# A memory-attention and sticky-routing expert kernel: values of batch 1 loaded ahead of the choice, their products split around the first w1 products

## The chip, the cores and the metric

The kernel runs on one core of a Trainium2 chip. The time is the device time of one execution in microseconds (us); lower is better. The core has five engines that run side by side, each in its own program order: TensorE (PE, with its weight loads shown as PEld), VectorE (DVE), ScalarE (ACT), GpSimd (POOL) and SyncE (SP), which here only issues transfers. An engine waits at an instruction until the semaphores that the instruction names have come, and everything behind it on that engine waits with it. Transfers between HBM and the on-chip memory go through DMA queues that SP fills; nearly all go through one.

## What is computed

The reference is a linear-attention step whose output goes through a sparse expert layer, for 8 batches of 8 heads, 576 tokens, head size 64, 32 memories, 8 experts with a hidden size of 1024. Cut to what matters:

```python
a = exp(phi - max(phi, axis=2)); a = a / (sum(a, axis=2) + 1e-9)
k_m = einsum('bhsm,bhsd->bhmd', a, k)
v_m = einsum('bhsm,bhsd->bhmd', a, v)
scores = q @ k_m.T / sqrt(64)
attn = softmax(scores)                     # over the 32 memories
x = (attn @ v_m), heads side by side       # (B, 576, 512)
logits = x @ w_gate
# token s keeps the expert of token s-1 when its local gate is 0.5 or more, token 0 takes the best
out[b, s] = softmax(logits[b, s])[e] * (relu(x[b, s] @ w1[e]) @ w2[e])
```

Because of the rule on the previous token, the tokens of one batch mostly share the expert that token 0 chose. The kernel therefore runs each batch once through that one expert; pairs of a batch and a further expert are listed at the end and done in a loop, which is passed over with these inputs.

## The kernel before

The work of a batch has two halves. The attention half turns `phi` into weights (column maximum `cm`, turned and reduced to `mc`, spread back as `cx`, subtracted, exponential, column sums `asum`), multiplies them with keys and values (`pkv`, line 396, 72 small products in 64x32 tiles of PE, keys and values side by side), adds the column sums (`f_sums`, line 407, into the same PSUM tiles), scales and turns the result (`kvn`, `pT`, `kvT`), and then treats the queries in two parts of 9 blocks of 32 tokens, called a and z: turn the queries (`qT`), scores (`psc`), softmax on DVE and ACT (`sc`), turn the weights back (`at`), and split them into a coarse and a fine part (`ah` on ACT, `al` on POOL). The choice of the expert (`c_pl`, `c_choice`) needs only token 0; `expert` reads the number into SP, and only then can w1 and w2 of that expert be asked for.

The expert half folds the values' means into w1 (`pg`, line 787, then `Gh` on ACT and `Gl` on DVE), multiplies (`hidden`: `ph`, line 819, 6 products for each 128 hidden units, relu'd by ACT and DVE into `h`) and multiplies with w2 (`second` and `second_turned`: `po`). The `ph` tiles and the `pg` tiles share three PSUM buffers, so a tile waits until DVE has read the one three before it. `hidden` runs four tiles of 256 tokens for two chunks each, then eight tiles of 320 tokens.

While the expert half of batch b runs on PE, the attention half of batches b+1 and b+2 is strewn between its products. Where, is written in the table `PLACES`: for each step and batch a place on a time axis of the products alone (37.8 units for each batch); a step is issued on all its engines, SP included, when the loop has passed that place. I call the expert half of batch b stage b: stage 0 runs from about 28 us, stage 2 from about 138 us.

The first attention half has nothing to hide behind. `start` writes its order out by hand: all of batch 0's attention, the load of batch 1's `phi` and keys and values, part of batch 1's attention, and `warm(n)`, n dummy products on PE, where PE would stand idle. The first `pg` runs in two halves (`lo` and `hi`), for whose input w1's first half is loaded in two pieces.

Two more rules set waits. `at` has one buffer, so DVE can write the next batch's `at` only after the store `att_d` of the last one has read it. And the loads of keys and values, of `phi`, and of the queries have one buffer each.

## Time and profile before

| what | value |
|---|---|
| three runs | 414.85, 415.64, 418.31 us; median 415.64 us |
| the profiled execution | 416.56 us, span from first to last instruction 414.8 us |
| granted clock of TensorE, mean | 0.999 of full speed |
| PE busy | 95% of the span |
| DVE, ACT, POOL busy | 69%, 43%, 36% of the span |
| moved by DMA | 82.58 MB, 199 GB/s over the span |

The profile is one execution. "Busy" is the time in which an engine worked on an instruction; matmuls overlap, so a busy PE need not be at its peak. A wait is put down to what came last. Since PE is the fullest engine, idle time of the others costs nothing as long as PE does not wait for them.

### The profile page before, as it was taken

Reading aid. Unit: us, or ns where it says so; the run is one execution under the profiler, and the core shown is the slowest. Engines: PE = TensorE matmul, PEld = TensorE weight load, DVE = VectorE, ACT = ScalarE, POOL = GpSimd, SP = SyncE. Lnnn points to the kernel's source line nnn. Section 1 sums busy time; section 2 is a strip of 40 time slices with the busy share of each in tenths; the row PEclk is TensorE's granted clock in tenths of the full one; section 3 lists DMA queues with packets and bytes.
Section 4 is the critical chain, followed back from the end, with each engine's and each line's share of the span. In section 5 each row is a group of like instructions: output and inputs, shape, how many; then the busy total and the mean of one; then the engine's idle time right before and its main releaser. Section 6 shows DMA issues by size and latency. Waiting matters only on the chain.

```text
span 414.8 us, 10606 instructions
## 1 busy us (share of the span) xinstructions
PE 395.0 (95%) x4195; PEld 326.7 (79%) x4195; DVE 284.4 (69%) x714; ACT 177.8 (43%) x427; POOL 150.9 (36%) x162
## 2 busy tenths in 40 slices
PE   8778898999999989999999999999999999999994
PEld 2546866798777977699778997789878996899884
DVE  4487788878976797886759767777757676625300
ACT  2154652436442744435541564336541564146010
POOL 3024541536241744038510681029410660156000
PEclk9999999999999999999999999999999999999999
DMA  8969793999197939798789198965974087202011
GB/s 238 286 224 291 167 372 122 199 283 378 31 351 127 371 131 246 174 379 299 228 162 399 37 300 152 297 244 164 241 134 170 2 246 253 82 0 65 25 40 55
DMA packets 115445, 82.58 MB, mean 199 GB/s; under 512 B 69616, under 2 KB 89088, under 8 KB 115392
## 3 DMA queue, kind: packets, MB, share of 16 engines
q1 hardware_dynamic: 115328, 81.84, 66.4%
q8 instruction: 35, 0.57, 0.6%
q14 instruction: 18, 0.15, 0.1%
q0 software_dynamic: 64, 0.02, 0.1%
HBM read 66.60 MB, written 15.24 MB: 197 GB/s over the span
## 4 chain that ended last, share of the span: by engine, by line
PE 79%; DMA 11%; DVE 5%; issue 1%; SPq 1%; ACT 1%; DVEq 0%
PE ph L819 22%; PE po L907 8%; PE po L857 8%; PE po L908 7%; PE po L909 7%; PE po L859 7%; PE po L858 7%; DMA att_d<-at 6%; DMA kv_t<-in_v_dram 5%; PE pkv L396 4%; PE pg L787 3%; PE psc L507 2%; PE pl L604 1%; DVE h L829 1%; PE po L881 1%
## 5 line engine op out<-in xcount | busy, mean ns | idle before, releaser
L777 POOL TENSOR_TENSOR w2l<-raw,w2h 128x512 fp32r<-128x512 f32 x64 | 82.0, 1303 | 31.2 <-ACT w2h L776 23.5
L819 PE MATMUL ph<-ah,Gh 128*128 128x256 f32 (+1 forms) x256 | 74.5, 306 | 1.4 <-DVE h L829 1.3
L829 DVE SCALAR_TENSOR_TENSOR h<-ph,h 128x320 fp32r<-128x320 f32 (+2 forms) x104 | 52.7, 519 | 31.9 <-ACT h L827 31.5
L819 PE MATMUL ph<-ah,Gl 128*128 128x256 f32 (+1 forms) x256 | 71.6, 295 | 0.0
L907 PE MATMUL po<-h,w2l 128*128 128x320 f32 x224 | 71.5, 319 | 0.0
L909 PE MATMUL po<-h,w2h 128*128 128x320 f32 x224 | 69.2, 309 | 0.0
L908 PE MATMUL po<-h,w2h 128*128 128x320 f32 x224 | 69.2, 309 | 0.0
L827 ACT ACTIVATE h<-ph 128x320 fp32r<-128x320 f32 (+1 forms) x96 | 46.4, 489 | 44.7 <-PE ph L819 44.4
L857 PE MATMUL po<-w2h,h 128*128 128x512 f32 (+1 forms) x152 | 60.7, 399 | 0.0
L914 POOL TENSOR_TENSOR oT<-oT,gT 128x320 f32<-128x320 f32 x28 | 20.7, 741 | 104.3 <-DVE oT L913 97.4
L859 PE MATMUL po<-w2h,h 128*128 128x512 f32 (+1 forms) x152 | 57.8, 380 | 0.0
L858 PE MATMUL po<-w2l,h 128*128 128x512 f32 (+1 forms) x152 | 57.7, 379 | 0.0
L819 PE MATMUL ph<-al,Gh 128*128 128x256 f32 (+1 forms) x256 | 54.8, 295 | 0.0
L819 PEld LDWEIGHTS ph<-ah,Gh 128*128 128x128 f32 x256 | 48.1, 188 | 7.6 <-issue 3.6
L819 PEld LDWEIGHTS ph<-ah,Gl 128*128 128x128 f32 x256 | 48.2, 188 | 0.0
L563 POOL TENSOR_TENSOR al<-at,ah 128x576 fp32r<-128x576 f32 (+1 forms) x18 | 23.1, 1289 | 64.7 <-ACT ah L559 42.8
L907 PEld LDWEIGHTS po<-h,w2l 128*128 128x128 f32 x224 | 42.0, 188 | 5.6 <-issue 5.2
L776 ACT ACTIVATE w2h<-raw 128x512 fp32r<-128x512 f32 x64 | 38.4, 625 | 11.9 <-PE po L909 10.1
L908 PEld LDWEIGHTS po<-h,w2h 128*128 128x128 f32 x224 | 42.1, 188 | 0.2
L909 PEld LDWEIGHTS po<-h,w2h 128*128 128x128 f32 x224 | 42.1, 188 | 0.0
L819 PEld LDWEIGHTS ph<-al,Gh 128*128 128x128 f32 x256 | 41.1, 188 | 0.1
L857 PEld LDWEIGHTS po<-w2h,h 128*128 128x128 f32 x152 | 28.6, 188 | 14.3 <-issue 9.4
(153 smaller groups left out, 578.6 us busy)
## 6 DMA issues: line engine op xcount, KB each, us to landing
raw<-in_moe_w_dram SPq DMA_DIRECT2D x34, 512.0 KB, 6.2
raw<-in_moe_w_dram SPq DMA_DIRECT2D x15, 1024.0 KB, 6.9
kv_t<-in_k_dram SPq DMA_DIRECT2D x7, 1152.0 KB, 8.7
kv_t<-in_v_dram SPq DMA_DIRECT2D x7, 1152.0 KB, 11.2
q_t<-in_q_dram SPq DMA_DIRECT2D x112, 72.0 KB, 3.3
att_d<-at SPq DMA_DIRECT2D x8, 576.0 KB, 9.8
out_dram<-oT SPq DMA_DIRECT2D x28, 160.0 KB, 5.6
out_dram<-ot SPq DMA_DIRECT2D x17, 256.0 KB, 6.0
```

The lines of the kernel that those rows point to most:

```text
L563: (eng or nc.gpsimd).tensor_tensor(out=st.al[:, gs, ss], in0=st.at[:, gs, ss], in1=st.ah[:, gs, ss], op=ALU.subtract)
L776: nc.scalar.activation(h, src, AF.Copy)
L777: nc.gpsimd.tensor_tensor(out=l, in0=src, in1=h, op=ALU.subtract)
L819: nc.tensor.matmul(pv[:, c - c0], lhsT=lt[:, g, cs], rhs=rt[:, g, s0 : s0 + n], start=(i == 0), stop=(i == 5),)
L827: nc.scalar.activation(hc[:, :, 0:n], pv, AF.Relu)
L829: nc.vector.scalar_tensor_tensor(out=hc[:, :, o : o + z - a], in0=pv[:, :, a:z], scalar=0.0, in1=hc[:, :, a:z], op0=ALU.max, op1=ALU.subtract,
L857: nc.tensor.matmul(po[:, c0:c1], lhsT=h[:, c, th], rhs=hi, start=(c == 0), stop=False)
L858: nc.tensor.matmul(po[:, c0:c1], lhsT=h[:, c, th], rhs=lo, start=False, stop=False)
L859: nc.tensor.matmul(po[:, c0:c1], lhsT=h[:, c, tl], rhs=hi, start=False, stop=(c == FC - 1))
L907: nc.tensor.matmul(po[:, 0:n], lhsT=lo, rhs=h[:, c, 0:n], start=(c == 0), stop=False)
L908: nc.tensor.matmul(po[:, 0:n], lhsT=hi, rhs=h[:, c, 0:n], start=False, stop=False)
L909: nc.tensor.matmul(po[:, 0:n], lhsT=hi, rhs=h[:, c, n : 2 * n], start=False, stop=(c == FC - 1))
```

## The change

It has five parts: the values of batch 1 are asked for right behind its keys, before the choice, and no longer behind w1; 40 of the 72 products `pkv` of batch 1 go in front of the first `pg` and the other 32 in front of the third, while seven `warm` products go; the column sums become one product for each half of the heads instead of four; the query load of a batch is two steps; and many entries of `PLACES` are new. The scores of batch 0's part z take their PSUM tiles from another pool (`ps_o`), since `pkv` now holds those of `ps_a` from earlier on. `c_pl` and `c_choice` go in front of `f_pm` and `f_mc` of batch 1.

```diff
-    def fetch_q(st):
+    def fetch_q(st, hs):
-        st.qt = pin.tile([P, HG, NB, 32], F32, tag="q", name="q_t", bufs=1)
+        if hs.start == 0:
+            st.qt = pin.tile([P, HG, NB, 32], F32, tag="q", name="q_t", bufs=1)
...
-        for h in range(HG):
+        for h in range(HG)[hs]:
...
     def f_sums(st):
-        for h in range(HG):
-            for g in range(NG):
-                nc.tensor.matmul(
-                    st.pkv[g][32 * h : 32 * h + 32, P : P + 1],
-                    lhsT=st.asum[half[g], h],
-                    rhs=ones[half[g]],
...
+        for g in range(NG):
+            nc.tensor.matmul(
+                st.pkv[g][:, P : P + 1],
+                lhsT=st.asum[half[g]].rearrange("p h m -> p (h m)"),
+                rhs=ones[half[g]],
...
     def k_psc(st, p):
-        pool, tag = (ps_h, "ph") if st.b == 0 and not hf else (ps_a, "pa")
+        pool, tag = (ps_a, "pa") if st.b else ((ps_h, "ph"), (ps_o, "po"))[hf > 0]
...
-        "pkv": f_pkv,
+        "pkv": lambda st: f_pkv(st, slice(5 if st.b == 1 else 0, TN)),
...
-        "q": fetch_q,
+        "q 0": lambda st: fetch_q(st, h),
+        "q 1": lambda st: fetch_q(st, w),
...
     def start():
         f_sums(s)
-        fetch_kv(n, (0,))
+        fetch_kv(n)
...
-        f_pm(n)
-        warm(3)
-        f_mc(n)
         c_pl(s)
         c_choice(s)
+        f_pm(n)
+        f_mc(n)
         expert(s)
         load1(s, 0, 2)
         load1(s, 1)
-        fetch_kv(n, (1,))
         load2(s, 0)
...
         for i in range(2):
             f_exp(n, i)
-        warm(3)
         for f in steps[4:]:
             f(s, p)
         k_ah(s, 0, PB)
+        f_pkv(n, slice(0, 5))
         lo, hi = slice(0, 256), slice(256, 512)
         w_pg(s, 0, lo)
         k_turn(s, z)
         w_G(s, 0, lo)
         k_al_each(s, 0, PB)
         f_asum_tree(n)
-        warm(1)
         w_pg(s, 0, hi, ps_o)
```

Two entries of the table, for the manner of it (the queries' one row of places becomes two):

```diff
-    "w2 1": {0: 3.6, 1: 33.2, 2: 67.2, 3: 102.7, 4: 132.8, 5: 169.8, 6: 207.6, 7: 243.4},
+    "w2 1": {0: 1.45, 1: 33.2, 2: 67.2, 3: 100.7, 4: 132.8, 5: 169.8, 6: 207.6, 7: 244.8},
-    "q": {1: 1.15, 2: 22.6, 3: 59.6, 4: 88.7, 5: 124.3, 6: 162.1, 7: 199.9},
+    "q 0": {1: 0.05, 2: 22.6, 3: 59.6, 4: 88.7, 5: 124.3, 6: 162.1, 7: 199.9},
+    "q 1": {1: 1.46, 2: 22.6, 3: 59.6, 4: 88.7, 5: 124.3, 6: 162.1, 7: 199.9},
```

What this does to the order on the engines is shown at three places. The first is SP's queue from batch 1's keys on, before; `kv_t` is keys or values, `raw` is w1 (first three) and w2, `q_t` the queries, `att_d` the store of `at`:

```order
L231 DMA kv_t<-in_k_dram 128x4x576
L1040 TENSOR_LOAD ei
L755 DMA raw_416<-in_moe_w_dram 128x4x256
L755 DMA raw_419<-in_moe_w_dram 128x4x512
L231 DMA kv_t<-in_v_dram 128x4x576
L765 DMA raw_422<-in_moe_w_dram 128x2x512
L253 DMA q_t<-in_q_dram 32x18x32 x16
L231 DMA phi_t<-in_phi_dram 128x4x288
L765 DMA raw_722<-in_moe_w_dram 128x2x512
L231 DMA kv_t<-in_k_dram 128x4x576
L231 DMA kv_t<-in_v_dram 128x4x576
L572 DMA att_d<-at 128x1152
```

The same stretch of SP's queue in the changed kernel (a piece of w1 or w2 that is loaded in two transfers stands once here, as above):

```order
L232 DMA kv_t<-in_k_dram 128x4x576
L232 DMA kv_t<-in_v_dram 128x4x576
L1041 TENSOR_LOAD ei
L756 DMA raw_408<-in_moe_w_dram 128x4x256
L756 DMA raw_411<-in_moe_w_dram 128x4x512
L766 DMA raw_413<-in_moe_w_dram 128x2x512
L255 DMA q_t<-in_q_dram 32x18x32 x8
L766 DMA raw_665<-in_moe_w_dram 128x2x512
L255 DMA q_t<-in_q_dram 32x18x32 x8
L232 DMA phi_t<-in_phi_dram 128x4x288
L232 DMA kv_t<-in_k_dram 128x4x576
L573 DMA att_d<-at 128x1152
```

The values stand ahead of the choice's number (`ei`), and the second piece of w2 between the halves of the queries; the store of `at` still stands behind all of them.

The second place is PE from the scores of batch 0's part z to the third `pg`, before; `wp` are the dummy products (three pairs ahead of the first `pg`, one ahead of the second), and the `ph` rows of a tile repeat:

```order
L507 MATMUL psc<-qT,kvT 32x288 x8
L305 LDWEIGHTS wz
L305 MATMUL wp<-wz 128x512
...
L787 MATMUL pg<-raw_416,kvT 32x256 x8
...
L787 MATMUL pg<-raw_416,kvT 32x256 x8
L819 MATMUL ph<-ah,Gh 128x256
...
L819 MATMUL ph<-al,Gh 128x256 x2
L787 MATMUL pg<-raw_419,kvT 32x512 x8
```

The same stretch of PE in the changed kernel:

```order
L508 MATMUL psc<-qT,kvT 32x288 x8
L398 MATMUL pkv<-kv_t,phi_t 32x128 x40
L788 MATMUL pg<-raw_408,kvT 32x256 x16
L820 MATMUL ph<-ah,Gh 128x256
...
L820 MATMUL ph<-al,Gh 128x256 x2
L398 MATMUL pkv<-kv_t,phi_t 32x128 x32
L788 MATMUL pg<-raw_411,kvT 32x512 x8
```

The 72 products `pkv`, which stood two tiles of `ph` further on, are in the two gaps ahead of the `pg`; the column sums now stand alone behind the second tile of `ph`, in front of the third.

The third place is DVE in stage 2, from the column maximum `cm` on, before; `h` is DVE's half of the relu of a `ph` tile, the rows `sm` to `at` are a softmax of batch 3:

```order
L310 TENSOR_REDUCE cm<-phi_t 128x128
L829 SCALAR_TENSOR_TENSOR h_2252<-ph,h_2252 128x320
L543 TENSOR_REDUCE sm<-sc 128x18
L829 SCALAR_TENSOR_TENSOR h_2252<-ph,h_2252 128x320
L546 TENSOR_SCALAR sm<-sm 128x18
L547 RECIPROCAL sm<-sm 128x18
L829 SCALAR_TENSOR_TENSOR h_2252<-ph,h_2252 128x320
L551 TENSOR_TENSOR sc<-sc,sm 128x576
L829 SCALAR_TENSOR_TENSOR h_2252<-ph,h_2252 128x320
L555 STREAM_TRANSPOSE at<-sc 128x2x288
```

The same stretch of DVE in the changed kernel:

```order
L312 TENSOR_REDUCE cm<-phi_t 128x128
L830 SCALAR_TENSOR_TENSOR h_2221<-ph,h_2221 128x320 x2
L544 TENSOR_REDUCE sm<-sc 128x18
L547 TENSOR_SCALAR sm<-sm 128x18
L548 RECIPROCAL sm<-sm 128x18
L552 TENSOR_TENSOR sc<-sc,sm 128x576
L830 SCALAR_TENSOR_TENSOR h_2221<-ph,h_2221 128x320
L556 STREAM_TRANSPOSE at<-sc 128x2x288
```

The second `h` now stands ahead of the sum, and the third behind the product of the softmax and no longer ahead of it. On ACT in stage 0 `kvT` of batch 1 stands ahead of the exponential `ex` and no longer behind it.

## Rows read from the trace of the kernel before

**Rows 1.** The page's first part: busy time, share of the span, instructions.
```profile
PE 395.0 (95%) x4195; PEld 326.7 (79%) x4195; DVE 284.4 (69%) x714; ACT 177.8 (43%) x427; POOL 150.9 (36%) x162
```
**Rows 2.** Waits of PE: who waited <- for what: us in total, times, longest.
```profile
PE pg L787 <- DMA raw<-in_moe_w_dram: 3.1, 3, 1.4
PE pkv L396 <- DMA kv_t<-in_v_dram: 1.7, 2, 1.4
PE pl L578 <- DVE at L555: 1.6, 2, 1.1
PE pgg L453 <- ACT kvT L440: 1.4, 1, 1.4
PE ph L819 <- DVE h L829: 1.3, 1, 1.3
...
PE psc L507 <- issue: 0.8, 1, 0.8
PE psc L507 <- DVE qT L480: 0.8, 1, 0.8
```
**Rows 3.** Stretches: length, busy PE, PEld, DVE, ACT, POOL, clock, DMA share, GB/s.
```profile
19.00:22.00 3.00, 3.00 (x48) 2.23 (x56) 1.88 (x10) 1.78 (x5) 0.00 (x0) 1.00 1.00 381
22.00:25.00 3.00, 3.00 (x56) 2.30 (x47) 2.69 (x9) 1.25 (x3) 1.00 (x1) 1.00 0.02 6
25.00:30.00 5.00, 2.71 (x45) 0.86 (x52) 4.43 (x9) 3.39 (x8) 0.54 (x1) 1.00 0.95 289
...
38.00:47.00 9.00, 8.91 (x134) 7.99 (x115) 5.94 (x15) 6.06 (x15) 6.76 (x6) 1.00 0.73 111
```
**Rows 4.** Timeline of SP: start, length, line, transfer, how many.
```profile
16.11 1.50 SPq L231 DMA_DIRECT2D kv_t<-in_k_dram  x1
23.89 1.56 SPq L755 DMA_DIRECT2D raw<-in_moe_w_dram  x3
...
50.16 1.01 SPq L572 DMA_DIRECT2D att_d<-at  x1
```
**Rows 5.** The page's DMA issues: how many, KB each, median us to landing.
```profile
kv_t<-in_v_dram SPq DMA_DIRECT2D x7, 1152.0 KB, 11.2
```
**Rows 6.** Timeline of PE around the first `pg`: start, length, what, wait before.
```profile
21.68 0.25 PE L578 MATMUL pl<-ggt,at 128*1 128x8 f32 x4
...
22.45 0.44 PE L355 MATMUL pm<-ident,mc 128*64 128x128 f32 x4
...
28.38 0.67 PE L787 MATMUL pg<-raw,kvT 64*32 64x256 f32 x16 [1.39 <-DMA raw<-in_moe_w_dram]
...
33.44 1.09 PE L787 MATMUL pg<-raw,kvT 64*32 64x512 f32 x16 [1.29 <-DMA raw<-in_moe_w_dram]
...
36.45 2.25 PE L396 MATMUL pkv<-kv_t,phi_t 64*32 64x128 f32 x144 [0.29 <-DMA kv_t<-in_v_dram]
38.62 0.39 PE L819 MATMUL ph<-ah,Gh 128*128 128x256 f32 x1
```
**Rows 7.** Timeline of DVE and ACT in stage 0.
```profile
22.72 0.14 DVE L597 TENSOR_SCALAR ei<-c 1x1 int32<-1x1 f32 x1
...
36.39 1.28 DVE L799 TENSOR_TENSOR Gl<-pg,Gh 128x512 fp32r<-128x512 f32 x2
...
63.21 0.78 DVE L555 STREAM_TRANSPOSE at<-sc 128x576 f32<-128x576 f32 x1 [0.94 <-DMA att_d<-at]
...
35.00 0.69 ACT L538 ACTIVATE sc<-sc 128x576 f32<-128x576 f32 x1 [2.21 <-DVE sc L534]
...
48.70 0.32 ACT L643 ACTIVATE ex<-ex 32x144 f32<-32x144 f32 x1 [0.50 <-DVE ex L640]
```
**Rows 8.** Timeline of DVE in stage 2, behind the column maximum.
```profile
149.62 0.43 DVE L829 SCALAR_TENSOR_TENSOR h<-ph,h 128x320 fp32r<-128x320 f32 x1
149.97 0.75 DVE L551 TENSOR_TENSOR sc<-sc,sm 128x576 f32<-128x576 f32 x1
```
**Rows 9.** Timeline of PE: the sums of a later batch, all records.
```profile
303.41 0.29 PE L407 MATMUL pkv<-ones,asum 64*32 64x1 f32 x16
```

28 lines of the change are left out of this document (14 added, 14 removed), and 82 rows, old and new, of the table PLACES.

## Prediction

> **What bounds the kernel now.** I read the page first: PE is busy 95% of the span [rows 1], so only what PE waits for, or work taken from PE, can be won. Then the list of who PE waited for [rows 2]: these seven entries sum to 10.7 us, and by the timeline all but 1.8 us of them (the 1.3 us behind `h`, and 0.5 of the 1.6 us of `pl`) lie in the first 65 us. So I look at three places: the queue of loads at 17 to 30 us, PE at 21 to 39 us, and the DVE row in which 1.3 us are lost at 148 us. After 65 us PE runs nearly without gaps, so a microsecond gained before stays gained, and one lost later stays lost.
>
> The stretches of the DMA queue [rows 3] show the hole that the change uses: while batch 1's keys come in (19 to 22 us) the queue moves 381 GB/s, then 6 GB/s for three microseconds until the choice is made and w1 is asked for at 23.89 [rows 4], then 289 GB/s. Behind it, from 38 to 47 us, the queue is 73% busy but moves only 111 GB/s (the small packets of the queries).
>
> **The change, part by part.** *Values in front.* 1152 KB are 1.18 MB, at 381 GB/s 3.1 us: 22.0 to 25.1 us. w1's bytes began to flow at about 25 us anyway. So I cost this load at nothing; the idle queue covers it, and if the cover fails, w1 is late (a rival below).
>
> *Choice in front of `pm`.* PE's three warm-up products stand before `pl` at 21.68 [rows 6]; without them `pl` follows the query turns, at about 21.2, and `ei`, ready at 22.86 (22.72 + 0.14) [rows 7], is some 0.5 us earlier. w1 is asked for at 23.4, but its bytes still begin where the values end, 25.1: no gain, no loss. In return `mc` waits for `ei`, so `pm` (22.45 [rows 6]) goes out at about 22.6, and the query turns, the softmax and G of batch 0 behind it are 0.2 us later.
>
> *Products of the values.* All 72 take 2.25 us at 36.45, after a wait; the next `ph` begins at 38.62 [rows 6]. Of them 40 (40/72 of 2.25 = 1.25 us) now run after the last `psc` and the exponentials, from about 26.8 to 28.1, where PE waited for w1 until 28.38; 32 (1.0 us) run in front of the `pg` at 33.44, where it waited 1.3 us for w1's other half. Both are covered by waits for w1 (3.1 us in three waits [rows 2]). What is late next: the `ph` tile at 38.62 needs the second half of Gl, which DVE makes at 36.39 in two instructions of 0.64 us [rows 7]; they stand behind a sum that needs ACT's exponential of 35.00, 0.69 long. That chain hangs on DVE and ACT and does not move, but for the 0.2 us of `mc`. The tile also reuses the PSUM buffer that the first of the two Gl frees at 37.03. So it starts at 37.2, not at 38.62: 1.4 us of the 2.5 are won, the rest is a new wait for Gl. The sums, which stood between the next two tiles (0.29 us [rows 9], of which I count 0.2, since their ends overlap the next product), now lie inside that wait, and I let 0.1 us of waiting for buffers go with it: 1.7 us at the first tile of 320. Bounds: 1.0 (Gl a further 0.7 late) to 2.5.
>
> *ACT order.* `ex` (48.70, 0.32 long) no longer stands in front of `kvT` [rows 7], for which `pgg` waits 1.4 us [rows 2]. I take 0.2, between 0 and 0.7 (all of that wait that lies behind `ex`). The second query turn moves ahead of one `h`: PE's 0.8 us wait for `qT` [rows 2] loses 0.1, at most 0.4.
>
> *Queue order.* DVE's `at` at 63.21 waited 0.94 us for the store of batch 0's `at` [rows 7], issued at 50.16 [rows 4], and PE's `pl` waited 1.1 for it [rows 2]. In front of the store now lie 3.1 us less (the values went early), and the second half of w2 goes between the two halves of the queries, into the stretch of 111 GB/s. So the store lands more than 3 us earlier, DVE needs it some 2.0 us earlier (1.7 + 0.2 + 0.1): the wait goes, 0.9 us. Bounds 0 and 1.1.
>
> *Stage 2, by the new table.* Behind the long column maximum of that stage DVE served three `h` with a sum between; the third began at 149.62, in front of the 0.75 us product [rows 8]. Now two `h` come first and the third stands behind that product: at 150.3 to 150.5. `ph` has three buffers and PE waits 1.3 us there for `h` [rows 2], so the tile that reuses the third buffer is that much later; later `h` catch up a little. I take a loss of 0.5 us, between 0 and 0.9.
>
> *Sums by group.* 16 matmul records of 0.29 us in all [rows 9] become 4 with a stationary operand of 128 columns. Four records with 1 column take 0.25 (`pl`), four with 64 columns and 128 moving ones 0.44 (`pm`) [rows 6]: between 0.04 won and 0.15 lost each, times 8; or, if only the count matters, 0.2 won each. I take nothing: range 1.2 lost to 1.6 won. The Trainium skill, "TensorE: Matmul & The Clock Gate", section "LDWEIGHTS (loading the stationary operand)", says the same in another way: a load's time goes with its columns, not its rows, P/1.2 ns; by it 16 loads of 32 columns and 4 of 128 cost an equal 0.43 us (an estimate), and the sum would not change.
>
> *The rest of the table* moves rows by one step where PE has no wait; cover is PE's own stream, and I cost it at nothing. A gap of 0.8 us in which PE waits for "issue" inside the first `psc` [rows 2] delays the choice; PE issues 24 records fewer before it, so it may fall behind that `psc` (0 to 0.4 us won). I take nothing.
>
> **Sum.** 1.7 + 0.2 + 0.1 + 0.9 - 0.5 = 2.4 us. The profiled execution took 416.56, so 414.2; the median of the three runs, 415.64, lies 0.9 below it: 413.2.
>
> **Rivals.** *The wait only changes its name:* batch 0's softmax ends later than I think, Gl 0.7 us late, and the store still binds `at`: 1.0 + 0.3 - 0.5 = 0.8 to 1.2 won, 414.6. For it speaks that every step from 28 to 38 us on DVE waits for ACT; against it, that only 0.2 us are added to that chain.
>
> *More is won:* stage 2 keeps its time, the issue gap leaves the choice's path, and the sums give 0.1 each: 2.4 + 0.5 + 0.35 + 0.8 = 4.05, so 411.6. For it: `h` in stage 2 has three buffers to catch up in; against: three independent things must go well.
>
> *w1 comes late (the other side):* a value load takes 11.2 us from issue to landing in the middle [rows 5]. Issued at 17.6, behind the keys (16.11 + 1.50 [rows 4]), it would land at 28.8; w1's first piece, which needs 28.38 - 25.1 = 3.3 us behind it, at 32.1, 3.7 us late. Then all of 28 to 38 us moves by 3.7, the 1.7 becomes a loss of 2.0, the rest (1.2 - 0.5) stays: 1.3 slower, 416.9. It decides from a delay of 2.4 us on. Against it: the 11.2 us come from queues that were full, and this one is empty.
>
> *The clock falls:* seven warm-up products are taken out. In the rows of before the granted clock is 1.00 in every stretch, also in those of 22 to 30 us with PE busy 2.71 of 5 us [rows 3], and the new waits (1.2 us at most by the above) are no longer than those it went through. If it did fall to 1.2 GHz there, those 2.71 us of work would take as much again, and over twice that stretch 5.4 us more: 418.6. The Trainium skill, "TensorE: Matmul & The Clock Gate", section "What's actually happening", holds that the default state is the throttled one and only activity releases it; by that rule taking warm-up work out is the risk here, but the trace shows no fall yet.
>
> **How the numbers follow.** The forecast has a chance of 0.55 (411.9 to 414.4 by the bounds of Gl, `at` and stage 2), the renamed wait 0.20, more won 0.15, late w1 0.07, clock 0.03. The range of 8 in 10 takes in both neighbours and the bounds of the sums: 410.8 ("more is won" with 0.2 for each of the sums) to 416.2 (the renamed wait with the sums 1.2 dearer is 415.8; the rest is part of a late w1). About 1% (4.2 us) is what a measurement of this kernel can tell from no change. Faster by over 1% (below 411.5) is half of "more is won" and a thin tail of the forecast: 0.11. Slower by over 1% (above 419.8) needs the clock or a later w1 still: 0.03. Within 1%: 0.86.
>
> **What would show it.** In the changed profile: the queue moves some 380 GB/s from 22 to 25 us; the first `pg` starts within 0.3 us of 28.4; `pkv` has no wait; PE shows a new wait for DVE's Gl of about a microsecond near 36 us; the first `ph` of 320 columns starts 1.7 us earlier than before; `at` no longer waits for the store; the third `h` behind the column maximum of stage 2 starts after the product. Wrong is the forecast if the first `pg` starts after 30 us, if the `ph` after the sums starts without a wait at 36 us, or if the gain read at 65 us (2.9 us) does not survive to the end but for stage 2.

## The result, and the profile after

The changed kernel is slower: 420.26 us (median of 20 runs, 417.91 to 425.40) against 416.82 us (20 runs, 414.85 to 418.85), ratio 1.0086 with a 95% interval of 1.0062 to 1.0110. Forecast were 413.2 us, 410.8 to 416.2. Its first profiled execution (span 423.5 us) had TensorE at half clock for 17 us in three stretches before the end, so the rows of after come from a second run of the same file, after_again (419.01 us, span 417.2; median of its 9 runs 420.19). That span is 2.45 us above the 414.8 us of before, and this is the difference that is explained below. The medians lie 3.4 us apart. Of the 71 runs of before with a mean granted clock of 0.994 or more the median is 416.5 us, of the 7 such runs of the changed kernel 419.05, 2.5 us more.

The page of after_again, busy time, and the queue of PE's instructions (packets, MB, share):

```profile
PE 397.8 (95%) x4090; PEld 328.3 (79%) x4092; DVE 286.3 (69%) x714; ACT 176.9 (42%) x427; POOL 150.2 (36%) x162
...
q8 instruction: 34, 0.56, 0.6%
```

PE has 105 records of products and 103 of loads fewer than before [rows 1] and is busy 2.8 us longer. Its waits (us in total, times, longest) answer to [rows 2]:

```profile
PE psc L508 <- DVE qT L481: 2.1, 1, 2.1
PE pl L605 <- issue: 2.1, 1, 2.1
PE ph L820 <- DVE h L830: 1.9, 2, 1.3
...
PE pkv L398 <- ACT phi_t L372: 1.1, 1, 1.1
PE pkv L398 <- issue: 0.6, 1, 0.6
PE pgg L454 <- ACT kvT L441: 0.6, 1, 0.6
```

The waits for w1 are gone, and the waits of `pl` for `at` fell from 1.6 us to 0.2; the wait for `kvT` fell from 1.4 to 0.6 us. In their place stand a wait for `qT` of 2.1 us (0.8 before), one of `pl` for "issue" of 2.1 us, which before did not have, and two for `h` instead of one.

To see where the difference arises, I took in both traces the start of the same product, counted over all `ph` and `po` products, whose order is the same. Forecast is the difference by the prediction's steps.

| product | before | changed | difference | forecast | head_sums (below) |
|---|---|---|---|---|---|
| first `ph` | 30.35 | 30.79 | +0.43 | 0 | 30.00 |
| first `ph` of 320 columns | 43.06 | 41.71 | -1.34 | -1.7 | 40.81 |
| `po` behind the `psc` that waits for `qT` | 55.92 | 56.35 | +0.43 | -2.0 | 55.45 |
| `po` behind the `pl` of batch 1 | 64.31 | 63.55 | -0.76 | -2.9 | 62.64 |
| `ph` that waits for `h` in stage 2 | 148.32 | 146.98 | -1.34 | -2.9 | 147.53 |
| 44 products later | 158.15 | 157.52 | -0.63 | -2.4 | 158.07 |
| 28 products later | 170.57 | 172.41 | +1.84 | -2.4 | 170.17 |
| end of the span | 414.77 | 417.22 | +2.45 | -2.4 | 414.47 |

**The start.** Stretches of after_again (columns as in [rows 3]), then PE's timeline (start, length, what, wait before):

```profile
22.00:25.00 3.00, 2.54 (x40) 2.26 (x40) 2.93 (x5) 1.66 (x5) 1.00 (x1) 1.00 1.04 394
25.00:27.00 2.00, 0.81 (x24) 0.30 (x32) 1.66 (x5) 1.71 (x4) 0.00 (x0) 1.00 1.09 350
27.00:31.00 4.00, 4.00 (x113) 2.48 (x113) 2.61 (x6) 1.39 (x4) 1.96 (x3) 0.57 1.07 379
```
```profile
26.91 2.12 PE L398 MATMUL pkv<-kv_t,phi_t 64*32 64x128 f32 x80 [1.09 <-ACT phi_t L372]
28.68 2.18 PE L788 MATMUL pg<-raw,kvT 64*32 64x256 f32 x32
...
33.46 0.95 PE L398 MATMUL pkv<-kv_t,phi_t 64*32 64x128 f32 x50 [0.63 <-issue]
...
41.71 0.41 PE L820 MATMUL ph<-ah,Gh 128*128 128x320 f32 x1
...
43.36 0.41 PE L820 MATMUL ph<-al,Gh 128*128 128x320 f32 x1 [0.35 <-POOL al L564]
```

The queue's hole at 22 us is filled (394 instead of 6 GB/s), the first `pg` starts at 28.68 without a wait, and the first tile of 320 columns 1.34 us earlier. The two parts of `pkv` in front of the `pg` do wait: 1.09 us for ACT's exponentials, which was forecast as a start at 26.8 us, and 0.63 us for "issue". TensorE did fall to 1.2 GHz, from 27.3 to 30.7 us (granted clock 0.57 in the mean of the third row), behind a stretch with PE busy 0.81 of 2 us.

**From 38 to 64 us.** DVE's timeline of after_again, then POOL's:

```profile
38.39 1.74 DVE L552 TENSOR_TENSOR sc<-sc,sm 128x576 f32<-128x576 f32 x1
...
53.32 1.27 DVE L705 TENSOR_TENSOR pr<-pe,es 32x18 f32<-32x18 f32 x1
...
54.92 0.76 DVE L481 STREAM_TRANSPOSE qT<-q_t 128x576 f32<-128x576 f32 x1
...
61.80 0.78 DVE L556 STREAM_TRANSPOSE at<-sc 128x576 f32<-128x576 f32 x1
```
```profile
38.23 1.29 POOL L778 TENSOR_TENSOR w2l<-raw,w2h 128x512 fp32r<-128x512 f32 x1 [4.52 <-ACT w2h L777]
...
53.28 4.98 POOL L778 TENSOR_TENSOR w2l<-raw,w2h 128x512 fp32r<-128x512 f32 x4 [6.23 <-ACT w2h L777]
```

Two DVE products of two SBUF operands begin 0.16 and 0.04 us behind the start of a product on POOL and end only behind its end: `sc` 0.6 us behind it, which makes it 1.74 us long instead of 0.76, and `pr`, with 18 columns, 0.03 us behind it, 1.27 us instead of 0.17. Behind `sc` stand `at`, `ah` and `al`; PE waits for that `al` at 43.4 us (the last row of the timeline above), and 0.9 us of what was won are gone there. `qT`, which stands behind `pr`, is late by it, and PE waits 2.1 us. `at` no longer waits for the store, as forecast.

The kernel before has such a meeting too, at another place; its DVE, then its POOL:

```profile
57.71 1.75 DVE L534 TENSOR_TENSOR sc<-sc,mx 128x576 f32<-128x576 f32 x1
```
```profile
53.84 5.00 POOL L777 TENSOR_TENSOR w2l<-raw,w2h 128x512 fp32r<-128x512 f32 x4 [6.94 <-ACT w2h L776]
```

In after_again the same `sc` takes 0.76 us, so that on the way to `at` DVE got back nearly the whole microsecond that `pr` had cost it.

**At 165 us.** PE's timeline, and the instruction packets of PE's queue (q8) that began from 143 to 144.5 and from 162 to 164 us; from 144.5 to 162 us none did:

```profile
159.88 2.25 PE L398 MATMUL pkv<-kv_t,phi_t 64*32 64x128 f32 x144
162.06 0.74 PE L605 MATMUL pl<-at,ggt 128*32 128x160 f32 x13
164.90 0.41 PE L605 MATMUL pl<-at,ggt 128*32 128x128 f32 x3 [2.10 <-issue]
```
```profile
q8 instruction: 1, 0.02, 4.5%
...
q8 instruction: 1, 0.02, 4.7%
```

PE stops in the middle of a `pl` whose inputs are all there. Its counts of records in that time:

```profile
143.40:162.00 18.60, 16.65 (x239) 13.35 (x237) 17.15 (x32) 9.20 (x19) 8.59 (x7) 1.00 0.68 227
162.00:164.85 2.85, 0.80 (x23) 0.42 (x14) 0.80 (x1) 0.00 (x0) 0.85 (x1) 1.00 0.59 72
```

Counted by their starts, PE ran 500 records between the packet at 143.4 us and the stop (the counts above add up to 513, since a record that crosses the edge of a stretch stands in both), and in that time no packet for it began until after 162 us. The page has 34 packets for 8,182 records, 241 each. So PE had run through about two packets' worth, and the next was late. The Trainium skill, "Runtime: NRT & Kernel Launch", section "Instruction fetch mechanics", says that an engine's sequencer gets its next 256 instructions over a DMA queue of its own while it executes, and that crossing such a boundary is mostly hidden. At this place the trace agrees with about two such blocks (488 to 500 records in the seven profiles that stop here; not with the 2,048 instructions that the page gives PE); hidden it was not. It is no fixed count: the stop of head_sums at 124 us comes after 548 records, and stops near 33 us in other profiles after 345 to 407.

**The sums.** A `pkv`, the sums behind it and the next `po`, of the changed kernel and then of before:

```profile
209.25 2.25 PE L398 MATMUL pkv<-kv_t,phi_t 64*32 64x128 f32 x144
211.43 0.39 PE L408 MATMUL pkv<-ones,asum 64*128 64x1 f32 x4
211.74 0.50 PE L858 MATMUL po<-w2h,h 128*128 128x512 f32 x1
```
```profile
207.46 2.25 PE L396 MATMUL pkv<-kv_t,phi_t 64*32 64x128 f32 x144
209.45 0.29 PE L407 MATMUL pkv<-ones,asum 64*32 64x1 f32 x16
209.68 0.50 PE L857 MATMUL po<-w2h,h 128*128 128x512 f32 x1
```

From the start of `pkv` to the next `po` it is 2.49 us with four sums and 2.22 with sixteen: 0.27 us lost, 0.19 of it already ahead of the first sum. Measured in the same way it is 0.27 to 0.29 us at the five places where a run of 64x32 tiles stands ahead (at 168 us against head_sums, since before has another order there), 0.12 at 86 and 128 us, where the sums stand between `po` products, and 0.31 in stage 0, 0.12 of that a wait: about 1.9 us in all, 1.4 of it behind 64 us. The sixteen sums have the tile shape of the `pkv` ahead of them and the four do not; that this makes the difference no run shows by itself. The Trainium skill, "TensorE: Matmul & The Clock Gate", section "LDWEIGHTS (loading the stationary operand)", lets a load's time go with its columns, so that by an estimate from it 16 loads of 32 and 4 of 128 would cost the same; the distances in PE's stream are not the same, and they decide.

### The profile page after: what moved, and what is told of

Its sections match the earlier page's. It is cut to its first block, busy times and chain, and to the rows that moved or that the text cites. A ratio compares the mean times of both kernels' runs of the same rounds, so it can differ in the third digit from the quotient of the medians.

```text
span 423.5 us, 10398 instructions
## 1 busy us (share of the span) xinstructions
PE 403.6 (95%) x4090; PEld 331.8 (78%) x4092; DVE 286.0 (68%) x714; ACT 176.8 (42%) x427; POOL 150.3 (35%) x162
## 4 chain that ended last, share of the span: by engine, by line
PE 82%; SPq 5%; DVE 5%; DMA 4%; issue 1%; ACT 0%; DVEq 0%
PE ph L820 19%; PE po L858 9%; PE po L908 9%; PE po L909 8%; PE po L910 8%; PE po L859 8%; PE po L860 8%; SPq L255 4%; PE pg L788 4%; PE pkv L398 4%; DMA kv_t<-in_v_dram 2%; PE psc L508 2%; DMA kv_t<-in_k_dram 2%; PE pl L605 1%; DVE h L830 1%
## 5 line engine op out<-in xcount | busy, mean ns | idle before, releaser
L858 PE MATMUL po<-w2h,h 128*128 128x512 f32 (+1 forms) x152 | 62.3, 410 | 0.0
L859 PE MATMUL po<-w2l,h 128*128 128x512 f32 (+1 forms) x152 | 59.4, 390 | 0.0
L860 PE MATMUL po<-w2h,h 128*128 128x512 f32 (+1 forms) x152 | 59.3, 390 | 0.0
```

Source lines behind the costliest of these rows:

```text
L858: nc.tensor.matmul(po[:, c0:c1], lhsT=h[:, c, th], rhs=hi, start=(c == 0), stop=False)
L859: nc.tensor.matmul(po[:, c0:c1], lhsT=h[:, c, th], rhs=lo, start=False, stop=False)
L860: nc.tensor.matmul(po[:, c0:c1], lhsT=h[:, c, tl], rhs=hi, start=False, stop=(c == FC - 1))
```

## The experiments

Three theories were set out: the clock falls where warm-up products were taken away (A), PE's instructions come late (B), or the new table loses time in many places (C). Ratios are to the kernel before, run on the same chip; its medians there were 416.6 to 417.8 us.

**The changed kernel again, with the warm-up products, and with the sums by head**

> The changed kernel once more, unaltered, to see which of the losses in its first profile come back. That profile (span 423.5 us) shows three stretches at half clock (from 26.7 us, 57.4 us and 166.6 us; 3.4, 3.4 and 10.2 us long) and one wait of 2.5 us of PE for its own instructions at 164.7 us. Theory A (the clock): the mean clock of most runs is 0.99, and a second profile shows falls at 26.7 and 57.4 us again, each costing about 1.7 us; the median is near 420. Theory B (instruction fetch): the 2.5 us wait at 165 us is there in every execution, since it hangs on the count of PE instructions ahead of it, and the clock falls only behind it. Theory C (the new table): neither comes back, and the time is lost in the many small waits of the later stages.

Measured: 420.19 us, ratio 1.0069 (1.0035 to 1.0104). The wait for instructions came back at the same `pl` (2.48 and 2.10 us), and so did the one for `qT`. Of the three stretches at half clock only the first came back. So B's wait and the one for `qT` belong to the program, while most of the falls of the clock come and go between its executions.

```diff
         f_pm(n)
+        warm(3)
         f_mc(n)
...
             f_exp(n, i)
+        wt[0] = ps_h.tile([P, 512], F32, tag="ph", name="wp")
+        warm(3)
...
         f_asum_tree(n)
+        warm(1)
```

> The changed kernel with the seven warm-up products put back at their three places (three in front of mc, three behind the exponentials of batch 1, one in front of the third pg). Theory A (the clock falls because PE stands idle where they were): no stretch at half clock at 26.7 us, the first pkv of batch 1 (1.25 us of work, 2.1 us at the low clock) at full speed, first ph tile about 1.2 us earlier than 30.74, time 1.5 to 2 us below the changed kernel. The fall at 57.4 us stays, since no product is put back there. Rival (the fall comes from the value products themselves, 80 small ones in a row): the fall stays, and the time is the same or 0.3 us longer.

Measured: 421.51 us, ratio 1.0109 (1.0064 to 1.0154), 1.3 us above the changed kernel. The stretch at half clock only moved, to 36.2 us, and the second `pkv` waited 1.90 us for "issue". The warm-up products did not bring the time back; whether they hold the clock up this run does not decide.

```diff
     def f_sums(st):
-        for g in range(NG):
-            nc.tensor.matmul(st.pkv[g][:, P : P + 1], ...
+        for h in range(HG):
+            for g in range(NG):
+                nc.tensor.matmul(st.pkv[g][32 * h : 32 * h + 32, P : P + 1], ...
```

> The changed kernel with the column sums by head as before (16 products instead of 4 for each batch). Theory B (instruction fetch): it has 12 more products and as many weight loads for each batch in front of 164 us, so PE's instruction fetch falls elsewhere: the 2.5 us wait at 165 us is gone or under 0.5 us, and so is the fall of the clock behind it; time 2 to 5 us below the changed kernel. Theory A: the clock falls at 26.7 and 57.4 us stay and the wait is a rare event; time within 1 us of the changed kernel, between 0.8 us lower and 1.2 us higher by what the sums themselves cost.

Measured: 416.77 us, ratio 0.9991 (0.9960 to 1.0022): 3.4 us below the changed kernel, and level with before. PE's timeline of head_sums at that place:

```profile
160.44 2.25 PE L398 MATMUL pkv<-kv_t,phi_t 64*32 64x128 f32 x144
162.62 0.74 PE L606 MATMUL pl<-at,ggt 128*32 128x160 f32 x16
```

No wait. By the table above the two profiles, 2.75 us apart at the end, part by 0.9 us up to 64 us and by 2.8 us from 158 to 171 us (the wait of 2.1 and one place of the sums lie there), and by 0.5 us behind that; between 64 and 158 us head_sums falls back by 1.5 us, and a smaller wait for instructions (0.70 us) appeared there inside a `pg` at 124 us. Theory C keeps what is left to the forecast of 413.2. In this profile the predicted wait for Gl is there as well, at the `ph` behind the sums:

```profile
36.71 0.38 PE L821 MATMUL ph<-ah,Gh 128*128 128x256 f32 x1 [1.21 <-DVE Gl L801]
```

**The kernel before without the warm-up products**

> The kernel before with only the seven warm-up products taken out; nothing is moved. Theory A (the products held the clock up): a stretch at half clock between 24 and 34 us, 3.4 us long; mean clock 0.995 instead of 0.999, time 1 to 2 us above the kernel before. Rival (the clock doesn't hang on them, but on the longer wait for the values in the changed kernel): clock 0.999, time within 0.3 us of the kernel before, since PE waits for w1 there in any case.

Measured: 416.31 us, ratio 0.9971 (0.9945 to 0.9996). The clock did fall (its runs have means of 0.975 to 0.994, their median 0.988; before has 0.983 to 0.999, median 0.995), and the median time did not rise. Its profile has half clock from 13.5 and from 30.6 us for 3.4 us each, of which the first lies ahead of all seven products. A stretch of that profile:

```profile
29.00:34.00 5.00, 4.07 (x44) 2.94 (x28) 2.74 (x7) 1.99 (x6) 3.51 (x4) 0.66 1.04 370
```

PE waits for w1 there (1.48 us ahead of the first `pg` and 0.33 ahead of the third, against 1.39 and 1.29 before [rows 6]); the slow work takes the place of the last of these waits. In this one profile the first tile of 320 columns is 0.9 us later than before, so a fall is not free there; in the medians no cost shows. So the two halves of A come apart: in the kernel before the products go with a higher clock, and no time is lost without them. For the changed kernel even the first half is not shown: the profile of head_sums, which lacks the same seven products, has no fall before its last 4 us, and the median of its mean clocks is 0.996.

**Theory B from three sides: the count of instructions**

The edit, in the kernel before:

```diff
     def f_sums(st):
-        for h in range(HG):
-            for g in range(NG):
+        for g in range(NG):
```

> The kernel before with the column sums by group, nothing else changed. In the changed kernel PE waits 2.1 to 2.5 us for its own instructions at 165 us, behind the 144 value and key products of a batch and while SP fills the queue with the small packets of the queries; with sums by head (head_sums) that wait is gone. Theory B (what counts is how many instructions stand ahead of that place): the kernel before with sums by group has nearly the count of the changed kernel there (60 products fewer than before, the changed kernel 64 fewer), so the wait of 2 to 2.5 us appears at about 163 us, and the time is 1.5 to 3 us above the kernel before. Rival D (the wait needs the new table, which moves SP's and PE's order against each other): no wait over 0.5 us there, time between 1.6 us below and 0.5 us above the kernel before.

Measured: 423.02 us, ratio 1.0120 (1.0076 to 1.0165), 5.2 us above before. The old table with the new sums has the wait, larger still, at the same `pl`; PE's timeline:

```profile
169.19 0.85 PE L603 MATMUL pl<-at,ggt 128*32 128x128 f32 x9 [3.56 <-issue]
```

Rival D falls: the table is not needed for it. The wait (3.6 us) and the sums (about 1.9) are together of the size of the 5.2 us; more is not shown, since the profile is the slowest of the six runs (426.31 us) and has half clock for 14 us in three stretches before the end.

```diff
     def warm(n):
-            nc.tensor.matmul(wt[0], lhsT=wz[:, 0:P], rhs=wz, start=True, stop=True)
+            for x in (slice(0, 256), slice(256, 512)):
+                nc.tensor.matmul(wt[0][:, x], lhsT=wz[:, 0:P], rhs=wz[:, x], start=True, stop=True)
```

> The changed kernel with each of its 36 warm-up products of the first 17 us cut into two of half the columns: the same columns in all, 72 PE instructions more (36 products and 36 weight loads), nothing else. Theory B: these 72 instructions move the place where PE runs out of instructions, so the 2.1 to 2.5 us wait at 165 us is gone or under 0.5 us, and the time is 1.5 to 3 us below the changed kernel, as with head_sums. Rival (the sums by group themselves cost time in every stage): the wait or the loss stays, time within 0.7 us of the changed kernel.

Measured: 420.90 us, ratio 1.0081 (1.0053 to 1.0110), no gain. The wait at 165 us is gone, as B expects, but another of 2.13 us stands among the warm-up products themselves at 16.7 us, and the start is lost by it; PE's timeline of warm_halves:

```profile
18.85 0.50 PE L308 MATMUL wp<-wz 128*128 128x256 bf16 x2 [2.13 <-issue]
...
166.00 0.74 PE L606 MATMUL pl<-at,ggt 128*32 128x160 f32 x16
```

So the place follows the count, and I was wrong that a moved wait is a wait less.

**Theory B: what the packet waits behind**

```diff
-    "q 0": {... 5: 124.3, ...
-    "q 1": {... 5: 124.3, ...
+    "q 0": {... 5: 129.6, ...
+    "q 1": {... 5: 129.6, ...
```

> The changed kernel with the query load of batch 5 asked for behind that batch's key and value products instead of ahead of them (its place 129.6 instead of 124.3); PE's instructions are the same in number and order. Theory B with the queue as its second half (instructions come late because the small query packets fill the DMA engines): the wait at 165 us shrinks from 2.1 to 2.5 us to under 0.7 us; the queries land some 5 us later, and if that is too late for their turn at about 182 us, a new wait of DVE's qT appears; time 1 to 2.5 us below the changed kernel. Rival (the instruction fetch alone is too slow for 288 short instructions in 2.25 us, whatever the queue does): the wait stays over 1.5 us.

Measured: 428.57 us, ratio 1.0254 (1.0209 to 1.0299). I had moved the wrong load: the queries in the queue at 155 to 170 us are those of batch 4. The wait at 165 us stayed (2.4 us), and DVE's `qT` of batch 5 cost PE 6 us of waits later. It decides nothing.

```diff
     def fetch_q(st, hs):
+        if st.b == 4:
+            st.qt = sts[3].qt
+            return
```

> The changed kernel without the 16 loads of the queries of batch 4, which fill the queue from 155 to 170 us with small packets; that batch is computed with the queries of batch 3 instead, so a part of the loads is left out. PE's instructions are the same in number and order. Theory B with the queue as its second half (PE's instructions are late because their packet stands behind the small packets): the wait for instructions at 165 us falls from 2.1 to 2.5 us to under 0.7 us, and the time by 1.5 to 2.5 us below the changed kernel. Rival (the fetch alone is too slow for 288 short instructions in 2.25 us, whatever the queue does): the wait stays over 1.5 us.

Measured: 422.97 us, ratio 1.0159 (1.0123 to 1.0195). The wait grew to 3.83 us. The small packets are not what it needs; without them SP issued the loads behind them at once. A stretch ahead of the wait, of no_q4:

```profile
160.00:164.00 4.00, 1.95 (x107) 1.43 (x93) 1.96 (x1) 1.07 (x2) 1.43 (x1) 1.00 1.05 391
```

The same, with w1 and the first half of w2 of batch 3 left out too:

```diff
     def w_load1(st, w1e, i, parts=1):
+        if st.b == 3:
+            st.raw1.append(zeros)
+            return
...
     def w_load2(st, w2e, i):
+        if st.b == 3 and i == 0:
+            st.raw2.append(zeros)
+            return
```

> The changed kernel without the loads that fill the queue at 153 to 170 us: w1 and the first half of w2 of batch 3 (zeros from the on-chip memory stand in for them, so that batch's result is left out) and the queries of batch 4 (those of batch 3 stand in). PE's instructions are the same in number and order. Without the queries alone (no_q4) the wait for instructions at 165 us grew from 2.1 to 3.8 us, while bulk loads at 375 to 392 GB/s took their place. Theory B with the queue as its second half, now of any kind: with the queue nearly empty at 158 to 164 us the wait falls to under 0.7 us. Rival (the fetch alone is too slow for 288 short instructions in 2.25 us, whatever the queue does): the wait stays over 1.5 us.

Measured: 418.02 us, ratio 1.0018 (0.9989 to 1.0047), 2.2 us below the changed kernel. Stretches of after_again, then stretches and PE's timeline of no_loads:

```profile
156.00:160.00 4.00, 4.00 (x26) 3.02 (x32) 3.11 (x6) 2.34 (x4) 2.83 (x2) 1.00 1.05 402
160.00:164.00 4.00, 2.80 (x157) 2.28 (x155) 2.80 (x2) 1.26 (x2) 1.43 (x1) 1.00 0.99 191
```

```profile
156.00:160.00 4.00, 4.00 (x20) 3.28 (x18) 3.11 (x6) 2.10 (x4) 2.83 (x2) 1.00 0.01 2
160.00:164.00 4.00, 3.37 (x161) 2.50 (x161) 3.22 (x3) 1.50 (x3) 1.42 (x1) 1.00 0.38 149
```
```profile
163.91 0.41 PE L616 MATMUL pl<-at,ggt 128*32 128x128 f32 x3 [0.63 <-issue]
```

With the DMA engines at 1% and 38% instead of full, the same instructions in the same order wait 0.63 us instead of 2.10. So a full queue, of large or small packets, makes the packet late. A full queue alone is not enough: head_sums has DMA shares of 0.95 and 1.06 in the same two stretches and does not wait, so the count of records ahead decides as well. That it is the 288 short records of a `pkv` (144 products and their loads in 2.25 us) that use up what PE has before the packet comes fits the place; no run changes them alone.

**DVE against POOL**

```diff
-    "split 0": {0: 2.5, ...
-    "split 4": {0: 11.6, ...
+    "split 0": {0: 3.5, ...
+    "split 4": {0: 12.75, ...
```

> The changed kernel with the first and the fifth split of w2 of batch 0 one step later (places 3.5 and 12.75 instead of 2.5 and 11.6), so that POOL's w2l no longer starts just ahead of two DVE products: the softmax product of batch 0 (1.56 us at 38.78 instead of 0.76 us) and the 32x18 product pr (1.26 us at 53.55 instead of 0.17 us), both of which end when POOL's instruction ends. Theory E (the DVE product waits until POOL has finished): both are back at 0.76 and 0.17 us, PE's wait for qT at 56 us falls from 2.1 to about 1 us and its wait for POOL's al at 43.5 us from 0.3 us to nothing; at 64 us the kernel is 1.2 to 1.9 us earlier than the changed one, and the end is 1 to 1.9 us earlier, if the instruction wait at 165 us stays what it is. Rival (the long DVE instructions are late instructions or a profile's mark): they stay long.

Measured: 418.68 us, ratio 1.0031 (0.9999 to 1.0063), 1.5 us below the changed kernel, though its interval overlaps that of after_again. DVE, then POOL, of no_clash:

```profile
38.58 0.76 DVE L552 TENSOR_TENSOR sc<-sc,sm 128x576 f32<-128x576 f32 x1
...
46.51 1.20 DVE L636 TENSOR_TENSOR t<-L,gmx 32x144 f32<-32x144 f32 x1
```
```profile
42.54 5.01 POOL L778 TENSOR_TENSOR w2l<-raw,w2h 128x512 fp32r<-128x512 f32 x4
```

The softmax product is back at 0.76 us, and `pr` at 0.17; the tile at 43.4 us no longer waits for `al`. But the four POOL products, now in a row, meet another DVE product at 46.51: 1.20 us, in after_again 0.29. So E holds for the mechanism, and the wait for `qT` fell only to 1.8 us. The forecast gain at 64 us is not in this profile (0.7 us later than after_again): it has half clock from 55.9 us and waits for instructions of 0.9 us at 19 and 1.2 us at 34 us. The Trainium skill, "SBUF — State Buffer", section "SBUF: two separate sides", has the rule: a DVE operation with two SBUF inputs and a GpSimd operation that reads SBUF exclude each other for a whole instruction. The two long rows of after_again, the one of before, the one of no_clash and the two of hs_qt_early (below) agree.

**The losses of the changed kernel taken out one by one**

On top of head_sums, the second query turn of batch 1 earlier:

```diff
-    "a qT 1": {1: 10.9, ...
+    "a qT 1": {1: 9.95, ...
```

> head_sums with one more edit: batch 1's second query turn (place 9.95 instead of 10.9) stands on DVE ahead of the eight instructions that end in pr, and no longer behind them. Theory E (the gain at the start is lost where DVE is late with qT, since pr waits for POOL): PE's wait for qT, 2.1 us at 54 us, falls to under 0.5 us, the products behind it start 1 to 1.6 us earlier, and so does the end: 1 to 1.6 us below head_sums. Rival (the h behind pr, late by 0.76 us, or the queries themselves take its place): a new wait of 0.8 us or more for h or for the load, gain under 0.5 us.

Measured: 417.65 us, ratio 1.0016 (0.9989 to 1.0043), nothing won. The wait for `qT` is gone and `po` stands at 52.64 us instead of 55.45, but `pl` then waits for `at` (1.6 us). DVE of hs_qt_early:

```profile
51.07 0.78 DVE L482 STREAM_TRANSPOSE qT<-q_t 128x576 f32<-128x576 f32 x1 [0.17 <-issue]
...
52.70 1.27 DVE L703 TENSOR_TENSOR ex<-ex,oh 32x144 f32<-32x144 f32 x1
...
54.33 0.83 DVE L706 TENSOR_TENSOR pr<-pe,es 32x18 f32<-32x18 f32 x1
...
61.85 0.78 DVE L557 STREAM_TRANSPOSE at<-sc 128x576 f32<-128x576 f32 x1 [0.35 <-DMA att_d<-at]
```

`at` starts at 61.85, in head_sums at 60.90: DVE now meets POOL twice (`ex` 1.27 us, 0.29 in head_sums, and `pr` 0.83, 1.27 in head_sums) and then waits 0.35 us for the store. Up to there DVE is the limit, and an earlier PE only waits in another place. A wait for instructions of 1.47 us at 34 us, which head_sums does not have, stands ahead of all that; the first tile of 320 columns is 0.7 us later than in head_sums.

On top of head_sums, five entries as before:

```diff
-    "colmax": {... 4: 80.5, ...
+    "colmax": {... 4: 80.6, ...
-    "a sum": {... 3: 82.5, ...
+    "a sum": {... 3: 82, ...
-    "a inv": {... 3: 82.5, ...
+    "a inv": {... 3: 83, ...
-    "a mul": {... 3: 82.5, ...
+    "a mul": {... 3: 83.7, ...
-    "a at": {... 3: 83.8, ...
+    "a at": {... 3: 84.5, ...
```

> The changed kernel with sums by head (head_sums, 416.8 us beside 416.9 of the kernel before), and with five entries of the table as they were (the column maximum of batch 4 and the sum, inverse, product and turn of batch 3's part a), so that DVE's third h behind the long column maximum stands ahead of the 0.75 us product again. Forecast of the prediction: this order costs 0.5 us (0 to 0.9); the trace of the changed kernel shows a second wait of 0.63 us for h at 151 us. If that is so, the second wait is gone, the kernel is 0.5 to 0.7 us earlier behind 152 us, and its time 0.5 us below head_sums. Rival (later h catch up): same time as head_sums.

Measured: 417.12 us, ratio 1.0009 (0.9977 to 1.0040): no difference to head_sums in the medians. In its profile the second wait for `h` is gone, and over the 44 products behind 148 us it loses 0.56 us against before, head_sums 0.72. So the order on DVE costs about 0.2 us, not 0.5; what the rest is stays open.

best1 has the edits of no_clash, hs_qt_early and hs_stage2 on top of head_sums, best2 the same without that of hs_qt_early. The lines of best1 that hs_stage2 does not have:

```diff
-    "a qT 1": {1: 10.9, ...
+    "a qT 1": {1: 9.95, ...
...
-    "split 0": {0: 2.5, ...
+    "split 0": {0: 3.5, ...
...
-    "split 4": {0: 11.6, ...
+    "split 4": {0: 12.75, ...
```

> head_sums with the edits of hs_stage2, hs_qt_early and no_clash together: the changed kernel with sums by head, the old order on DVE in stage 2, the early query turn, and two splits of w2 a step later. If the three losses are apart from each other: 0.6 by the order of stage 2, 1.2 by the query turn, 0.7 by the softmax product that no longer waits for POOL; together 2 to 2.5 us below head_sums, near 414.5 us where the kernel before has 416.9. If they cover each other, or the instruction fetch moves a wait to another place: 0 to 1.5 us below.

Measured: 416.65 us, ratio 0.9999 (0.9977 to 1.0021). The gains do not add up. Whether the edits cover each other stays open: the profile also has a wait for instructions of 1.92 us at 34 us, which head_sums does not have, and is 1.5 us behind head_sums at 64 us.

> The changed kernel with sums by head, the old order on DVE in stage 2 and two splits of w2 one step later (head_sums, hs_stage2 and no_clash together, without the early query turn, behind which PE only waited for at in place of qT). If the gains add: 0.6 by stage 2 and 0.5 to 0.9 by the softmax product that no longer waits for POOL, so 415.5 to 416 us where head_sums has 416.8 and the kernel before 416.9. If DVE is the limit up to 64 us, the second gain is lost there and 416.2 is left; a wait for instructions anywhere in it takes another 0.5 to 2 us.

Measured: 416.35 us, ratio 0.9994 (0.9971 to 1.0017). Its profile ends 1.0 us before that of before; the medians do not tell it from before.

**The parts of the change alone**

The values alone, in the kernel before (the scores' PSUM pool as in the changed one):

```diff
-    "pkv": {1: 1.56, ...
+    "pkv": {1: 0.01, ...
...
-        fetch_kv(n, (0,))
+        fetch_kv(n)
...
-        fetch_kv(n, (1,))
...
-        warm(3)
...
         k_ah(s, 0, PB)
+        f_pkv(n, slice(0, 5))
...
-        warm(1)
```

> The kernel before with the first part of the change alone: the values of batch 1 asked for behind its keys, 40 of the 72 products in front of the first pg and 32 in front of the third, four of the seven warm-up products out; sums by head, the table but for one entry, and the load of the queries as before. The prediction's first term (1.7 us at the first product tile of 320 columns), by itself. If the split does what the prediction said: that tile starts 1.2 to 1.7 us earlier than 43.06. Theory F (from 45 to 64 us DVE is the limit, and the gain is lost there): at the pl product at 64 us 0 to 0.9 us are left, and the end is 0 to 1 us below the kernel before. Rival (the whole gain stays): 1.5 to 2 us below. Instruction waits: PE has 8 records fewer than before, so no new wait is expected.

Measured: 418.10 us, ratio 1.0016 (0.9990 to 1.0041): no gain. The tile of 320 columns starts at 43.22 us, not earlier than before, since the first `ph` stops for instructions while w1 and w2 come in at 387 GB/s; PE's timeline:

```profile
33.41 0.28 PE L819 MATMUL ph<-ah,Gl 128*128 128x256 f32 x1 [1.96 <-issue]
```

That no new wait was to be expected with 8 records fewer was wrong. At 64 us the difference is +0.1. The expected gain was not seen, so this run says nothing on Theory F. It does show what the early values do to the store of `at`, with the queue's order as before; DVE's timeline has no wait there:

```profile
62.64 0.78 DVE L555 STREAM_TRANSPOSE at<-sc 128x576 f32<-128x576 f32 x1
```

The queue's order alone, on top of before_no_warm (the query load in halves as in the changed kernel):

```diff
-    "q": {1: 1.15, ...
+    "q 0": {1: 0.05, ...
+    "q 1": {1: 1.46, ...
-    "w2 1": {0: 3.6, ...
+    "w2 1": {0: 1.45, ...
```

> The kernel before without the seven warm-up products (before_no_warm, 416.3 beside 416.9 us), and with the queries of batch 1 loaded in halves, the second half of w2 between them. The values stay behind w1. In the kernel before PE waits 1.1 us at 64 us for at, and at 0.9 us for the store. If the order of the queue alone frees that store, the wait is gone: 0.9 us below before_no_warm, about 415.4. If it is the early values that free it (3.1 us less in the queue ahead of the store), the wait stays and the time is that of before_no_warm within 0.4 us.

Measured: 417.22 us, ratio 1.0001 (0.9982 to 1.0021), 0.9 us above the median of before_no_warm. The order of the queue alone wins nothing that can be measured, and in its profile the wait for the store stays:

```profile
65.06 0.78 DVE L557 STREAM_TRANSPOSE at<-sc 128x576 f32<-128x576 f32 x1 [1.50 <-DMA att_d<-at]
```

The store lands at 64.94 us here and at 64.56 in before_no_warm; with the early values alone (before_values) it lands at 57.82, in before at 63.08, in after_again at 59.68. So it is the early values that free the store, not the order of the queries and w2.

## Why the prediction was wrong

**Right.** *Values in front, products in the gaps*: the queue's hole is filled at 394 GB/s, the first `pg` starts at 28.68 (28.1 to 28.7 was asked for), and of 1.7 us at the first tile of 320 columns 1.34 came. The new wait for Gl of about a microsecond was not in after_again; there the second part of `pkv`, 0.63 us late, stood in its place. head_sums has it (1.21 us), and there 2.24 us came. *ACT order*: the wait for `kvT` fell by 0.8 (0.2 forecast), of which 0.4 arrived at the next `ph`. *Queue order*: `at` no longer waits for the store, which lands 3.4 us earlier (more than 3 forecast), but by the early values alone, as before_values and best3 show. *Stage 2* lost 0.7 over the next 44 products (0.5 forecast), though little of it by the order that I named.

**Wrong: the gap for "issue", "0 to 0.4 us won", "I take nothing".** Behind 65 us the prediction has PE's own stream as cover. That holds as long as PE has its instructions. The one entry of [rows 2] that says "issue" was in the prediction, with the thought that fewer records may move it, but only at the `psc` where it stood, and only for a gain. Fewer records by the sums move the place in every later batch, and one came to lie behind 288 short records under a full queue: 2.1 us. head_sums takes it away, before_group_sums makes it in the old kernel, no_loads shrinks it. The new table is not what makes it: head_sums has that table and no wait, before_group_sums has the wait without it.

**Wrong: sums by group, "I take nothing", 1.2 lost to 1.6 won.** They cost 1.9 us. The duration of four records, 0.39 us, was within the bounds; what was missed is that the sixteen small products take 0.29 us together [rows 9] *and* follow 0.19 us sooner on the `pkv` ahead of them, so a row's length was set against a row's length where the distance to the next `po` counts.

**Wrong: the sum of gains up to 65 us, 2.9.** 0.76 are there, and 1.66 in head_sums. The gains of PE were added up one behind the other, as if PE were the limit. At 43 us it is POOL's `al`, behind the `sc` that met POOL, which takes 0.9 us back; from 45 to 62 us it is DVE: the start of its chain behind `L` came 0.3 us earlier only (46.91 instead of 47.18), the change added 1.1 us to it where `pr` met POOL, and the 0.1 won for `qT` became 1.3 lost. Between there and 64 us 1.2 came back (0.9 forecast), and in part by luck: besides the store, the meeting of `sc` with POOL that before has at 57.71 us was gone.

**The rivals.** The clock did fall, but the fall at 27 us accounts for at most the 0.43 us by which the first `ph` is late; that the missing products are the reason is not shown for this kernel. Late w1 did not happen. No rival had the mechanism that decided.

Put together, by the steps of the first table, from -2.4 to +2.45 are 4.85 us. Up to the first tile of 320 columns 0.4 us less was won than forecast; from there to 56 us 1.8 were lost where 0.3 were to be won (`al` and `qT` above), which is 2.1 us; up to 64 us 0.3 more was won than forecast. From 64 to 148 us 0.6 was won where nothing was forecast; a wait for instructions of 0.47 us that before has inside a `pkv` at 127 us is gone there. Stage 2 lost 0.2 more. From 158 to 171 us 2.5 were lost, the wait of 2.1 and one place of the sums, and behind that 0.6 us, where three more of them lie.

Two things lie outside this. The forecast of 413.2 stood on three runs of before with a median of 415.64; 20 runs have 416.82, so 1.2 of the 7.1 us between forecast and measurement are the base. And the medians lie 1.0 us further apart than the two profiles; runs at a mean clock of 0.994 or more do not (2.5 us), so this part goes with the clock, but why the changed kernel has fewer such runs is not settled.

## What to carry to other kernels

When a change takes instructions away or adds them, look for the "issue" waits of the fullest engine and for runs of many short instructions under a full DMA queue: here the packets of instructions came late behind other transfers, and each edit that changed the count of instructions moved the place. Add up gains only as far as the same engine stays the limit; behind that, follow the next engine's chain and ask what moved its start, and what its operations now meet on other engines. And price an operation by the distance between its neighbours in a full stream, not by the length of its row.

## What the runs showed of the hardware

- At one `pl` PE stopped 488 to 500 records after its last packet of instructions had begun, and stood for 2.1 to 3.8 us in seven profiles of six kernels (DMA share 0.99 and 1.05 in after_again, 1.05 in no_q4); with shares of 0.01 and 0.38 (no_loads) it stood for 0.63 us.
- A DVE product of two SBUF operands that starts behind a POOL product ends only behind it: 1.27 instead of 0.17 us with 18 columns (0.03 us behind POOL's end), 1.74 instead of 0.76 with 576 (0.6 us behind it).
- Four records of products with 128-column loads and one moving column cost 0.27 us more in PE's stream than sixteen with 32-column loads where a run of 64x32 tiles stands ahead, and 0.12 between `po` products.
- Without seven warm-up products the kernel before had a median mean clock of 0.988 instead of 0.995, and no loss of time in the median (0.9971).
